# Column-tile streaming of the weights in the serial chain of a two-layer decode kernel

## The chip, the cores and the metric

The kernel runs on one core of one Trainium2 chip. The metric is device time of one execution in microseconds (us); three runs of the kernel before gave 1079.07, 1079.63 and 1081.63 us, a median of 1079.63 us. TensorE is called PE below, VectorE DVE, ScalarE ACT, GpSimd POOL, and SyncE, whose queue issues nearly all DMAs, SP. "PEld" is a weight load on PE: the stationary operand is loaded, then the moving operand is streamed past it.

## The reference

Two layers, each an attention block A over a cached K and V and a block B of small products, run one after the other on a single position of 8 batch rows. Both layers use the same cache and the same weights.

```python
B, Sq, D = 8, 1, 448;  Hq, Hkv, Sk, Dh = 16, 8, 4096, 256;  F = 1792
def _A_ref(x, k_cache, v_cache, wq, wo):
    q = (x @ wq) split into Hq heads of Dh
    scores = einsum("bhqd,bhkd->bhqk", q, k) * Dh ** -0.5   # k, v repeated to Hq heads
    o = einsum("bhqk,bhkd->bhqd", softmax(scores), v)
    return o.reshape(B, Sq, Hq * Dh) @ wo
def _B_ref(x, w1, w2, w3, w4):
    ...
    return x1 + _gelu(_layernorm(x1) @ w3) @ w4
x = A_x
x = x + _A_ref(_layernorm(x), A_k_cache, A_v_cache, A_wq, A_wo)
x = x + _B_ref(_layernorm(x), B_w1, B_w2, B_w3, B_w4)
x = x + _A_ref(_layernorm(x), A_k_cache, A_v_cache, A_wq, A_wo)
x = x + _B_ref(_layernorm(x), B_w1, B_w2, B_w3, B_w4)
```

With one position the shifts in block B move every column out of the row, so `hs` is zero, w1 and w2 drop out, and x1 is the block's own input, `_layernorm(x)`.

## The kernel before

**Work units.** A unit is a pass (0 for the first layer, 1 for the second), a batch row b and a pair of KV heads gp (0 to 3). Each unit has four K blocks and four V blocks of 1 MB; SBUF has 15 places of 1 MB for them (`NC = 15`). The second pass of a row reads the same cache as the first, so 12 of a row's 32 blocks stay in their places from pass 0 to pass 1 (`kept`: all K of gp 2 and 3, four V blocks), one more V block is parked in PSUM (`inner`) and a quarter of another (`part`). While a row's kept blocks wait for its second pass, three places are left through which other blocks stream.

**Order.** `block` and `first_kept` write out the order of all blocks (`items`). For a row, the two kept units of pass 0 come last before the turn to pass 1. Right after them come V blocks of other units that were saved up for this point: `items.extend(due[:n])`, with `AFTER = 11`. These are the `narrow` items; their loads are cut into two halves of 512 KB (`halved`). Rows 0 to 3 have 11 narrow V blocks here (they are also in `loose`), rows 4 to 7 have 10. Then come the scores of the same row's pass 1 with the kept K.

**The chain.** Between pass 0 and pass 1 of a row lies a serial chain for that row (`chain`, L499): `half` turns the attention output of the last two units into columns (o_sb copy L471, products L477, copy L481); `add_cols` multiplies by the second half of wo (L365, 64 products of a 128x128 weight block with a one-column vector); `norm` (DVE operations L227 to L302, a product with ones L235, a power on POOL L254); `mlp_hidden` with w3 (L383, 56 products) and gelu (L401 to L406); w4 (L365 again, 56); `norm` once more; `project_q` with wq (L316, 128) and the copy of q (L325); then `give_q` spreads q (L335, L339). In all these products the 128x128 block of the weights is the stationary operand and the vector is the moving one, so each output is a column with one number a partition, as the next step needs it.

**Interleaving.** The chain is a Python generator. `step` runs it to the next `yield` and so sets how its instructions stand between others in each engine's queue. In narrow items a step is taken after each half of a V block: `pv` (L847) issues 8 products of 128x8 weights with 256 moving columns, then comes a piece of chain, then the next 8. The four outputs of L847 stand on PSUM partitions 0, 32, 64 and 96, so four of them run in four column tiles of the array.

```python
            e["skip"] = got == 2 or (got == 3 and items[now[0]] in loose)
```

In narrow items `yield 0` goes straight on to the next piece, `yield 2` skips the next turn, and `yield 3` does so in loose items.

**Loads.** `emit_loads` issues a block's DMA (K L741 and L766, V L766, halves L769) when a place comes free; SP is one queue in order, and a half's DMA waits until PE has read what the place held.

**PSUM.** `sc` is the bank of the scores (L794, read by the exponentials L803 on ACT), `misc` holds the small results, `o` two accumulators of the attention output.

Of the kernel before, what the change touches and what calls it, by code (L numbers as in the profile page):

```python
# [17 lines left out]
def kernel(  # L18
# [72 lines left out]
    identb = consts.tile([128, 128], BF16, name="identb")  # L91
    nc.vector.tensor_copy(identb[:], ident)

    usel = consts.tile([128, 4], FP32, name="usel")
    for u in range(2):
        nc.vector.tensor_reduce(
            usel[:, 2 * u : 2 * u + 2],
# [10 lines left out]
        ALU.add,  # L108
    )

    ptz = consts.tile([128, 264], BF16, name="ptw")
    nc.vector.memset(ptz[:], 0.0)
    ptw = ptz[:, 0:256].rearrange("p (r n w) -> p r n w", r=2, w=8)
    psv_t = consts.tile([128, NP * 128], BF16, name="psv")
    psv = [
# [1 line left out]
        for k in range(NP)  # L117
    ]

    misc = psum.tile([128, 512], FP32, name="misc")  # L120
    ot_bank = misc[:, 256:288]
    sc = psum.tile([128, 512], FP32, name="sc")
# [15 lines left out]
        at, n = {"y": (0, 8), "st": (64, 2), "h": (80, HC), "q": (256, NB2)}[what]  # L138
        return store[0][:, at : at + n * nb]

    wv = consts.tile([128, 4], FP32, name="wv")
    nc.vector.memset(wv[:, 0:3], 1.0 / D)
    nc.vector.memset(wv[0:64, 3:4], 0.0)
    nc.vector.memset(wv[64:128, 3:4], 1.0 / D)
# [65 lines left out]
    def norm(x, nb, twice):  # L210

        def room(name, shape, at):
            n = shape[0] * shape[1]
            if nb < Bn:
                t = chn.tile([128, n * MID], FP32, tag=name)
                ap = t[:, 0 : n * nb]
            else:
                ap = scratch(at, n * nb)  # L220
            return ap.rearrange("p (s f b) -> p s f b", s=shape[0], f=shape[1])

        def bc(ap):
            return ap.unsqueeze(1).to_broadcast([128, 4, nb])

        xx = room("xx", (2, 4), 0)
        nc.vector.tensor_mul(xx[:, 0], x, wv[:].unsqueeze(2).to_broadcast([128, 4, nb]))  # L227
        nc.vector.tensor_mul(xx[:, 1], xx[:, 0], x)
        xs = room("xs", (1, 2), 512)[:, 0]
        nc.vector.tensor_reduce(  # L230
            xs, xx.rearrange("p s f b -> p s b f"), mybir.AxisListType.X, ALU.add
        )
        yield 3
        st = room_ps("st", nb).rearrange("p (s b) -> p s b", b=nb)
        nc.tensor.matmul(st, ones, xs, start=True, stop=True)  # L235
        yield 0
        mv = room("mv", (1, 2), 528)[:, 0]
        nc.vector.tensor_copy(mv, st)
        var = room("var", (1, 1), 608)[:, 0, 0]
        if nb == 1:  # L240
            nc.vector.scalar_tensor_tensor(
                var, mv[:, 0], mv[:, 0], mv[:, 1], ALU.mult, ALU.subtract, reverse1=True
            )
        else:
            nc.vector.tensor_mul(var, mv[:, 0], mv[:, 0])
            nc.vector.tensor_sub(var, mv[:, 1], var)

# [12 lines left out]

        if twice and nb == 1:
            nc.vector.scalar_tensor_tensor(
                ve[:, :, 0], var.to_broadcast([128, 2]), 0.0, eps2[:], ALU.max, ALU.add
            )
            power(0, 2)
        else:
            if twice:
                nc.vector.tensor_scalar(
                    ve[:, 1], var, 0.0, EPS * EPS / (1 + EPS), ALU.max, ALU.add
                )  # L270
                power(1, 2)
            nc.vector.tensor_scalar(ve[:, 0], var, 0.0, EPS, ALU.max, ALU.add)
            power(0, 1)
        xc = room("xc", (1, 4), 576)[:, 0]
        nc.vector.tensor_tensor(xc, x, bc(mv[:, 0]), ALU.subtract)  # L275
        yield 0
        if nb > 1:
            yield
        c = (1 + EPS) ** -0.5 if twice else 1.0
        rl = rs[:, n - 1]  # L280
        parts = ((0, 128, 0, 0, 3, 0), (0, 64, 64, 3, 4, 4), (64, 128, 64, 3, 4, 3))
        if nb == 1:
            nc.vector.scalar_tensor_tensor(
                xbs(1)[:, 0:4, 0], xc[:, :, 0], rl, low[:, int(twice)], ALU.mult, ALU.mult
            )
            parts = parts[1:2]
        for p0, p1, x0, f0, f1, to in parts:
            pp = slice(x0, x0 + p1 - p0)
            dst = xbs(nb)[p0:p1, to : to + f1 - f0, :]
            if nb == 1:  # L290
                nc.vector.tensor_scalar(dst, xc[pp, f0:f1], rl[pp], c, ALU.mult, ALU.mult)
            else:
                nc.vector.scalar_tensor_tensor(
                    dst,
                    xc[pp, f0:f1],
                    c,
                    rl[pp].unsqueeze(1).to_broadcast([p1 - p0, f1 - f0, nb]),
                    ALU.mult,
                    ALU.mult,
                )  # L300
# [43 lines left out]
    def y_room(nb):  # L344

        return room_ps("y", nb).rearrange("p (u f b) -> p u f b", u=2, b=nb)
# [29 lines left out]
    def mlp_hidden(b0, nb):  # L376

        yield from norm(xT[:, :, b0 : b0 + nb], nb, True)
        h_ps = room_ps("h", nb)
        for c in range(HC):  # L380
            for fc in range(4):
                w, xi = wblk(w3_sb, F, c, fc)
                nc.tensor.matmul(  # L383
                    h_ps[:, c * nb : c * nb + nb],
                    w,
                    xbs(nb)[:, xi, :],
                    start=(fc == 0),
                    stop=(fc == 3),
                )
            if c % 7 == 6:  # L390
                yield 0 if c == HC - 1 else None
        g_t = chn.tile([128, HC * MID], FP32, tag="g")
        hh = g_t[:, 0 : HC * nb]
        g0 = g_t[:, HC : 2 * HC] if nb == 1 else misc[:, 448 : 448 + HC * nb]
        if nb == 1:
            HT_t = chn.tile([128, HC, 1], BF16, tag="HT")
            HT = HT_t[:]
        else:
            HT = HTw[:, :, b0 : b0 + nb]

        nc.vector.tensor_scalar_mul(hh, h_ps, 0.5)  # L401
        nc.vector.scalar_tensor_tensor(g0, hh, 4 * 0.044715, hh, ALU.mult, ALU.mult)
        nc.vector.scalar_tensor_tensor(g0, g0, 1.0, hh, ALU.add, ALU.mult)
        nc.scalar.activation(g0, g0, ACT.Tanh, scale=2 * 0.7978845608028654)
        yield 0
        nc.vector.scalar_tensor_tensor(  # L406
            HT,
            g0.rearrange("p (c b) -> p c b", b=nb),
            1.0,
            hh.rearrange("p (c b) -> p c b", b=nb),  # L410
            ALU.add,
            ALU.mult,
        )
        yield 2
        return HT

    def mlp(b0, nb):
        HT = yield from mlp_hidden(b0, nb)
# [2 lines left out]
    def z_cols(zall, gps):  # L421
# [8 lines left out]
        nc.vector.tensor_tensor(  # L430
            zm[:],
            zs.unsqueeze(1).to_broadcast([128, 4, np_]),
            usel[:].unsqueeze(2).to_broadcast([128, 4, np_]),
            ALU.mult,
        )
        yield
# [12 lines left out]
                OT[:, j, h0 : h0 + 2], o_ps[:, j, h0 : h0 + 2], rz[:, 2 * u : 2 * u + 2, 0]  # L449
            )  # L450

    def half(o_ps, zall, gps, OT, ready):

        while locked:
            yield
# [11 lines left out]
        )  # L467
        while not ready():
            yield
        o_sb = chn.tile([128, Dh], FP32, tag="o_sb")  # L470
        nc.scalar.copy(o_sb[:], o_ps)  # L471
        yield
        nc.vector.memset(o_ps, 0.0)  # L473
        free_o.append(o_ps)
        ot_ps = ot_bank[:, 16 * g8 : 16 * g8 + 2 * n8].rearrange("p (j h) -> p j h", j=2)
        for j in range(2):
            nc.tensor.matmul(  # L477
                ot_ps[:, j], o_sb[:].rearrange("p (i j) -> p j i", j=2)[:, j], R, start=True, stop=True
            )
        yield 0  # L480
        nc.vector.tensor_copy(OT, ot_ps)  # L481
        locked.pop()
        yield

    locked = []
# [2 lines left out]
    def first_half(b, st, ready):  # L488
# [6 lines left out]
        xs = xT[:, :, b : b + 1]  # L495
        nc.vector.tensor_add(xs, xs, y_room(1)[:, 0])

    def chain(b, st, ready):
        OT = work.tile([128, 2, Hq // 2, 1], BF16, tag="OTb", bufs=1)  # L499
        yield from half(st["o", 1], st["z"], [2, 3], OT[:, :, :, 0], ready)  # L500
        yield from add_cols(
            y_room(1)[:, 1],
            lambda i: OT[:, i % 2, i // 2 - Hq // 2],
            wo_sb,
            range(NB2 // 2, NB2),
            2,
        )
        xs = xT[:, :, b : b + 1]
        nc.vector.tensor_add(xs, xs, y_room(1)[:, 1])
        yield from mlp(b, 1)  # L510
        qT = chn.tile([128, NB2], BF16, tag="qT2", bufs=2)
        yield from project_q(b, 1, qT[:].unsqueeze(2))
        state[1, b] = {"qT": qT}
        give_q((1, b))

# [445 lines left out]
    for idx, it in enumerate(items):  # L961
# [17 lines left out]
        if kv == 0:  # L979
# [32 lines left out]
                    scores(two[0], x, qbd, gp, between=turn)  # L1012
                    scores(two[1], x + 1, qbd, gp)
            if c == 1:
                p_n = work.tile([128, 4, 32, 4], BF16, tag="p_sb", bufs=1)
                p_of[n] = p_n
            if c % 2 == 1:
                exps(p_of[n], st["z"], gp, c // 2)
                if kept_now and c == 3:
# [152 lines left out]
```

## Time and profile before

| what | value |
|---|---|
| median of 3 runs | 1079.63 us |
| the profiled execution's own time | 1081.69 us |
| its span, first to last instruction | 1079.8 us |
| HBM read | 436.28 MB, 404 GB/s over the span |
| busy, share of the span | PE 61%, PEld 38%, DVE 57%, ACT 15%, POOL 2% |
| mean granted TensorE clock | 0.63 |
| chain products: L316 / L383 / L365 | 1024 / 448 / 1024 + 448 matmuls of one column |
| L847 | 3968 matmuls, 252.1 us busy, idle before them 116.5 us |
| L794 | 4896 matmuls, 246.6 us busy |

How to read it: "busy" is the time in which an engine executes; a line such as L847 is the line of the kernel that issued the instruction. The views used later are the page (totals, and the span in 40 slices), the chain of waits that ended last, the groups of instructions by line and form (busy time, mean duration of one in ns, idle time before them and what ended it), the timeline (start, duration, engine, line, operation, how many merged), the waits, and windows (busy time by engine in a chosen stretch, with the granted clock, the DMA share and GB/s).

### The profile page before, as it was taken

What the parts mean: (1) busy time and instruction counts of PE and PEld (TensorE: products, weight loads), DVE (VectorE), ACT (ScalarE), POOL (GpSimd) and SP (SyncE); (2) the same over time, 40 slices, a digit from 0 to 9 for tenths busy, and PEclk for the clock granted to TensorE, in tenths of its full rate; (3) what the DMA queues carried; (4) which work ended last, traced back from release to release, by engine and by line L of the source; (5) the groups of instructions that cost most, each with busy time, mean ns of one, the idle gap of its engine ahead of it and who ended that gap; (6) DMA issues with size and microseconds to landing.
All of it is one profiled execution on the core that took longest, in us unless ns stands there. A gap on an engine that the chain in (4) does not pass through costs nothing.

```text
span 1079.8 us, 29813 instructions
## 1 busy us (share of the span) xinstructions
PE 654.5 (61%) x13292; PEld 407.1 (38%) x13292; DVE 610.2 (57%) x1266; ACT 162.2 (15%) x612; POOL 16.3 (2%) x27
## 2 busy tenths in 40 slices
PE   3244458644776437764487537854776467756875
PEld 2122235422443214432254324532453245433554
DVE  4357841677426872368714773297429743874371
ACT  0001111111111111111112111111111111111110
POOL 0000000000000000000000000000000000000000
PEclk9999855656565565655556655665565556655665
DMA  9999999999999999999999999999999999999994
GB/s 359 394 425 425 425 407 390 424 424 424 389 393 426 424 423 396 407 426 422 422 394 420 421 425 397 393 426 426 410 395 425 424 407 399 425 424 406 393 419 179
DMA packets 69200, 438.22 MB, mean 406 GB/s; under 512 B 7368, under 2 KB 11344, under 8 KB 38736
## 3 DMA queue, kind: packets, MB, share of 16 engines
q1 hardware_dynamic: 68880, 435.94, 98.6%
q8 instruction: 104, 1.70, 0.6%
q10 hardware_dynamic: 192, 0.38, 0.1%
q14 instruction: 24, 0.20, 0.0%
HBM read 436.28 MB, written 0.01 MB: 404 GB/s over the span
## 4 chain that ended last, share of the span: by engine, by line
DMA 62%; PE 20%; DVE 11%; SPq 2%; issue 2%; ACT 2%; POOL 0%; DVEq 0%; ACTq 0%
DMA places<-in_A_v_cache_dram 35%; DMA places<-in_A_k_cache_dram 24%; PE o L847 7%; DVE places L779 7%; PE sc L794 6%; PE misc L365 2%; SPq L174 2%; PE misc L316 1%; DMA w_sb<-in_B_w_dram 1%; DVE store L814 1%; ACT p_n L803 1%; PE misc L477 1%; PE misc L383 1%; DVE places L821 1%; DMA wq_sb<-in_A_wq_dram 1%
## 5 line engine op out<-in xcount | busy, mean ns | idle before, releaser
L779 DVE STREAM_TRANSPOSE places<-places 128x512 uint32<-128x512 uint32 (+1 forms) x576 | 457.9, 855 | 127.7 <-DMA places<-in_A_k_cache_dram 125.7
L794 PE MATMUL sc<-places,qbd 128*8 128x256 bf16 (+1 forms) x4896 | 246.6, 352 | 243.2 <-DVE places L779 236.1
L847 PE MATMUL o<-places,ptw 128*8 128x256 bf16 x3968 | 252.1, 386 | 116.5 <-DMA places<-in_A_v_cache_dram 92.1
L794 PEld LDWEIGHTS <-qbd 128*8 128x8 bf16 x4896 | 129.2, 104 | 325.6 <-DVE places L779 145.9
L847 PEld LDWEIGHTS <-ptw 128*8 128x8 bf16 x3968 | 100.3, 101 | 184.7 <-issue 112.2
L803 ACT ACTIVATE p_n<-sc 128x256 bf16<-128x256 f32 x128 | 95.0, 742 | 381.6 <-PE sc L794 381.6
L957 ACT COPY ptw<-psv 128x32 bf16<-128x32 bf16 x248 | 52.7, 225 | 201.2 <-PE o L847 185.9
L837 ACT CAST psv<-misc 128x128 bf16<-128x128 f32 x64 | 17.0, 266 | 234.2 <-PE misc L830 234.2
L441 DVE RECIPROCAL rz<-misc 128x8 f32<-128x8 f32 (+1 forms) x35 | 6.6, 188 | 69.8 <-PE misc L438 69.8
L316 PEld LDWEIGHTS <-wq_sb 128*128 128x128 bf16 x1152 | 34.1, 104 | 27.2 <-issue 16.6
L365 PEld LDWEIGHTS <-wo_sb 128*128 128x128 bf16 x1280 | 37.8, 102 | 15.6 <-issue 15.4
L339 DVE CAST qbd<-misc 32x64 bf16<-32x64 f32 x104 | 22.4, 216 | 30.4 <-PE misc L335 29.4
L316 PE MATMUL misc<-xb,wq_sb 128*128 128x1 bf16 x1024 | 33.2, 166 | 3.1 <-issue 2.3
L477 PE MATMUL misc<-R_t,o_sb 128*128 128x8 f32 (+1 forms) x132 | 25.9, 305 | 13.4 <-ACT o_sb L471 7.1
L803 ACT ACTIVATION_READ_ACCUMULATOR p_n<-sc 128x1 f32 x128 | 33.6, 262 | 0.0
L365 PE MATMUL misc<-OT,wo_sb 128*128 128x1 bf16 x1024 | 31.5, 165 | 1.9 <-DVE OT L481 1.7
L477 PEld LDWEIGHTS misc<-R_t,o_sb 128*128 128x128 f32 x132 | 23.0, 245 | 24.4 <-ACT o_sb L471 14.2
L325 DVE CAST qT<-misc 128x32 bf16<-128x32 f32 x8 | 1.5, 191 | 51.8 <-PE misc L316 51.8
L254 POOL TENSOR_TENSOR t<-t,nhalf 128x2 f32<-128x2 f32 (+2 forms) x20 | 14.0, 703 | 1051.1 <-DVE t L275 1051.1
L473 DVE MEMSET o<- 128x256 f32 x33 | 9.0, 272 | 32.9 <-PE o L847 29.9
L830 PEld LDWEIGHTS <-p_n 128*128 128x128 bf16 x256 | 11.8, 105 | 31.5 <-issue 20.4
L830 PE MATMUL misc<-identb,p_n 128*128 128x32 bf16 x256 | 18.1, 191 | 8.1 <-ACT p_n L803 6.8
(107 smaller groups left out, 313.5 us busy)
## 6 DMA issues: line engine op xcount, KB each, us to landing
places<-in_A_k_cache_dram SPq DMA_DIRECT2D x65, 2048.0 KB, 19.1
places<-in_A_v_cache_dram SPq DMA_DIRECT2D x107, 1024.0 KB, 20.6
places<-in_A_v_cache_dram SPq DMA_DIRECT2D x202, 512.0 KB, 7.1
places<-in_A_k_cache_dram SPq DMA_DIRECT2D x62, 1024.0 KB, 13.2
places<-in_A_v_cache_dram SPq DMA_DIRECT2D x8, 768.0 KB, 14.3
wo_sb<-in_A_wo_dram SPq DMA_DIRECT2D x1, 3584.0 KB, 27.1
wq_sb<-in_A_wq_dram SPq DMA_DIRECT2D x3, 1024.0 KB, 9.7
w_sb<-in_B_w_dram SPq DMA_DIRECT2D x1, 1568.0 KB
```

Source lines behind the costliest of these rows:

```text
L174: nc.sync.dma_start(t[:, fc * cols : (fc + 1) * cols], src[fc * 128 : fc * 128 + 128, :])
L316: nc.tensor.matmul(q_ps[:, j * Hq + h, :], w, xbs(nb)[:, xi, :], start=(fc == 0), stop=(fc == 3),)
L339: nc.vector.tensor_copy(qbd[32 * a : 32 * a + 32, :, :, a, :], qs.rearrange("p e (f g u h) -> p (e f) u g h", f=2, u=2, h=2)[:, :, u],)
L365: nc.tensor.matmul(y_ps[:, fc, :], w[:, i, at : at + 128], rhs(i), start=start, stop=stop, skip_group_check=open is not None,)
L477: nc.tensor.matmul(ot_ps[:, j], o_sb[:].rearrange("p (i j) -> p j i", j=2)[:, j], R, start=True, stop=True)
L779: nc.vector.transpose(w, w)
L794: nc.tensor.matmul(sc[32 * k : 32 * k + 8, 128 * x : 128 * (x + nx)], qbd[:, ep, gp].rearrange("p a h -> p (a h)"), v, start=(n == 0), sto ...
L803: nc.scalar.activation(p_sb[:, :, :, 2 * u : 2 * u + 2].rearrange("p t i x -> p x t i"), sc[:, 256 * u : 256 * u + 256].rearrange("p (x t ...
L830: nc.tensor.matmul(pt_ps[:, t], p_sb[:, t].rearrange("p i x -> p (i x)"), cols, start=True, stop=True,)
L837: nc.scalar.copy(p_to, pt_ps.rearrange("p t k (a h) -> p a (t k) h", a=4))
L847: nc.tensor.matmul(o_ps[32 * q : 32 * q + 8, :], ptz[:, at : at + 8], v[:, y * Dh : (y + 1) * Dh], start=False, stop=(y >= 12), skip_group ...
L957: nc.scalar.copy(ptw[:, ring_of[it], :, 6:8], psv[slot_of[it[0]]][:, it[2]])
```

## The change

All of it is in the chain (`chain`); `first_half`, `rest` and the tail keep their products. The weights become the moving operand and the vector the stationary one, one column wide: a product gives a row on one PSUM partition. Four of them, on partitions 0, 32, 64 and 96 of the bank `sc`, run in four column tiles. wo's second half takes 16 products of 448 columns, w3 16 of 512 or 384 columns, w4 14 of 448, wq twice 16 of 512. After each such group DVE copies the bank to SBUF (`rows_out`, 128 x 448 or 512; for wq to bf16), and products with the copied rows as the stationary operand and a selection matrix as the moving one turn the rows into columns: for wo and w4 four fp32 products with `pick_all` (128x1, which also sums the four partial rows), for w3 four fp32 products with `pick` (128x4), for wq eight bf16 products with `pickb`. gelu works on 16 columns in place of 14.

Around it: one SBUF tile `buf` serves `o_sb`, the copied rows and the exponentials `p_of` in turn, and the lock that `half` takes is kept until wq's rows are turned (`hold=True`). The positions of the chain's yields change with the groups. The number of narrow items (`AFTER = 11`) and all loads stay.

```diff
+    nc.vector.tensor_copy(pick, ident.rearrange("p (q r) -> p q r", q=4)[:, :, 0])
...
+    pickb = ptz[:, 264:268]
+    nc.vector.tensor_copy(pickb, pick)
...
+    buf = consts.tile([128, 2 * Dh], FP32, name="buf")
...
+    nc.vector.tensor_reduce(pick_all, pick, mybir.AxisListType.X, ALU.add)
...
-    def half(o_ps, zall, gps, OT, ready):
+    def half(o_ps, zall, gps, OT, ready, hold=False):
...
-        o_sb = chn.tile([128, Dh], FP32, tag="o_sb")
-        nc.scalar.copy(o_sb[:], o_ps)
+        o_sb = buf[:, 0:Dh]
+        nc.scalar.copy(o_sb, o_ps)
...
-        locked.pop()
+        if not hold:
+            locked.pop()
...
+    def row(q, n):
+
+        return sc[32 * q : 32 * q + 1, 0:n]
+
+    def rows_out(n):
+
+        nc.vector.tensor_copy(buf[:, 0:n], sc[:, 0:n])
+
+    def sums(x, w, n, y_ps):
+
+        for i in range(n):
+            nc.tensor.matmul(
+                row(i % 4, D), x(i), w(i), start=i < 4, stop=i >= n - 4, skip_group_check=True
+            )
+        yield 0
+        rows_out(D)
+        yield
+        for fc in range(4):
+            nc.tensor.matmul(
+                y_ps[:, fc, :],
+                buf[:, min(128 * fc, D - 128) :][:, 0:128],
+                pick_all,
+                start=True,
+                stop=True,
+            )
+        yield 0
+
     def chain(b, st, ready):
         OT = work.tile([128, 2, Hq // 2, 1], BF16, tag="OTb", bufs=1)
-        yield from half(st["o", 1], st["z"], [2, 3], OT[:, :, :, 0], ready)
-        yield from add_cols(
-            y_room(1)[:, 1],
-            lambda i: OT[:, i % 2, i // 2 - Hq // 2],
-            wo_sb,
-            range(NB2 // 2, NB2),
-            2,
+        yield from half(st["o", 1], st["z"], [2, 3], OT[:, :, :, 0], ready, hold=True)
+        xs = xT[:, :, b : b + 1]
+        y_ps = y_room(1)[:, 1]
+        yield from sums(
+            lambda i: OT[:, i % 2, i // 2], lambda i: wo_sb[:, NB2 // 2 + i], NB2 // 2, y_ps
         )
-        xs = xT[:, :, b : b + 1]
-        nc.vector.tensor_add(xs, xs, y_room(1)[:, 1])
-        yield from mlp(b, 1)
+        nc.vector.tensor_add(xs, xs, y_ps)
+
+        yield from norm(xs, 1, True)
+        first, many = (0, 4, 7, 11), (4, 3, 4, 3)
+        for fc in range(4):
+            for q in range(4):
+                c, n = first[q], 128 * many[q]
...
+                nc.tensor.matmul(
+                    row(q, n),
+                    xbs(1)[:, xi, :],
+                    w,
+                    start=fc == 0,
+                    stop=fc == 3,
+                    skip_group_check=True,
+                )
+        yield 0
+        rows_out(512)
+        yield
+        h_ps = misc[:, 298:314]
+        for k in range(4):
+            nc.tensor.matmul(
+                h_ps[:, 4 * k : 4 * k + 4], buf[:, 128 * k : 128 * k + 128], pick, start=True, stop=True
+            )
+        yield 0
+        HT_t = chn.tile([128, 16, 1], BF16, tag="HT")
+        yield from gelu(h_ps, 16, 1, HT_t[:])
+        of = [4 * k + q for q in range(4) for k in range(many[q])]
+        yield from sums(lambda i: HT_t[:, of[i]], lambda i: w4_sb[:, i], HC, y_room(1)[:, 0])
+        nc.vector.tensor_add(xs, xs, y_room(1)[:, 0])
+
+        yield from norm(xs, 1, False)
+        q_ps = room_ps("q", 1)
+        rows = buf[:].bitcast(BF16)
+        for ph in range(2):
+            for fc in range(4):
+                for q in range(4):
...
+                    nc.tensor.matmul(
+                        row(q, 512),
+                        xbs(1)[:, xi, :],
+                        w,
+                        start=fc == 0,
+                        stop=fc == 3,
+                        skip_group_check=True,
+                    )
+            yield 0
+            nc.vector.tensor_copy(rows[:, 512 * ph : 512 * ph + 512], sc[:])
+            yield
+        for ph in range(2):
+            for k in range(4):
+                c = (k % 2) * Hq + 8 * ph + k // 2
+                nc.tensor.matmul(
+                    q_ps[:, c : c + 7 : 2],
+                    rows[:, 512 * ph + 128 * k : 512 * ph + 128 * k + 128],
+                    pickb,
+                    start=True,
+                    stop=True,
+                )
+        yield 0
+        locked.pop()
         qT = chn.tile([128, NB2], BF16, tag="qT2", bufs=2)
-        yield from project_q(b, 1, qT[:].unsqueeze(2))
+        nc.vector.tensor_copy(qT[:], q_ps)
+        yield
         state[1, b] = {"qT": qT}
         give_q((1, b))
...
-                p_n = work.tile([128, 4, 32, 4], BF16, tag="p_sb", bufs=1)
-                p_of[n] = p_n
+                p_of[n] = buf[:, Dh:].bitcast(BF16).rearrange("p (t i x) -> p t i x", t=4, i=32)
```

More of the change, by code (lines that the diff above doesn't have):

```diff
@@ L92 @@
     nc.vector.tensor_copy(identb[:], ident)
-    usel = consts.tile([128, 4], FP32, name="usel")
+    usel_t = consts.tile([128, 8], FP32, name="usel")
+    usel, pick = usel_t[:, 0:4], usel_t[:, 4:8]
     for u in range(2):
@@ L109 @@
     )
-    ptz = consts.tile([128, 264], BF16, name="ptw")
-    nc.vector.memset(ptz[:], 0.0)
+    nc.vector.tensor_copy(pick, ident.rearrange("p (q r) -> p q r", q=4)[:, :, 0])
+    ptz = consts.tile([128, 268], BF16, name="ptw")
+    nc.vector.memset(ptz[:, 0:264], 0.0)
+    pickb = ptz[:, 264:268]
+    nc.vector.tensor_copy(pickb, pick)
     ptw = ptz[:, 0:256].rearrange("p (r n w) -> p r n w", r=2, w=8)
@@ L139, in room_ps @@
         return store[0][:, at : at + n * nb]
-    wv = consts.tile([128, 4], FP32, name="wv")
+    wv_t = consts.tile([128, 5], FP32, name="wv")
+    wv, pick_all = wv_t[:, 0:4], wv_t[:, 4:5]
+    nc.vector.tensor_reduce(pick_all, pick, mybir.AxisListType.X, ALU.add)
     nc.vector.memset(wv[:, 0:3], 1.0 / D)
@@ L226, in norm @@
         xx = room("xx", (2, 4), 0)
-        nc.vector.tensor_mul(xx[:, 0], x, wv[:].unsqueeze(2).to_broadcast([128, 4, nb]))
+        nc.vector.tensor_mul(xx[:, 0], x, wv.unsqueeze(2).to_broadcast([128, 4, nb]))
         nc.vector.tensor_mul(xx[:, 1], xx[:, 0], x)
@@ L391, in mlp_hidden, with gelu @@
                 yield 0 if c == HC - 1 else None
+        HT = HTw[:, :, b0 : b0 + nb]
+        yield from gelu(h_ps, HC, nb, HT)
+        return HT
+    def gelu(h_ps, n, nb, HT):
         g_t = chn.tile([128, HC * MID], FP32, tag="g")
[L393 to L399, printed above, removed]
+        hh = g_t[:, 0 : n * nb]
+        g0 = g_t[:, n : 2 * n] if nb == 1 else misc[:, 448 : 448 + n * nb]
         nc.vector.tensor_scalar_mul(hh, h_ps, 0.5)
@@ L414, in mlp_hidden @@
         yield 2
-        return HT
     def mlp(b0, nb):
@@ L432, in z_cols @@
             zs.unsqueeze(1).to_broadcast([128, 4, np_]),
-            usel[:].unsqueeze(2).to_broadcast([128, 4, np_]),
+            usel.unsqueeze(2).to_broadcast([128, 4, np_]),
             ALU.mult,
@@ L477, in half @@
             nc.tensor.matmul(
-                ot_ps[:, j], o_sb[:].rearrange("p (i j) -> p j i", j=2)[:, j], R, start=True, stop=True
+                ot_ps[:, j], o_sb.rearrange("p (i j) -> p j i", j=2)[:, j], R, start=True, stop=True
             )
@@ new lines, in chain @@
+        xs = xT[:, :, b : b + 1]
+        y_ps = y_room(1)[:, 1]
+        yield from sums(
+            lambda i: OT[:, i % 2, i // 2], lambda i: wo_sb[:, NB2 // 2 + i], NB2 // 2, y_ps
+        )
+        nc.vector.tensor_add(xs, xs, y_ps)
[4 more added lines that the diff above has]
+                c, n = first[q], 128 * many[q]
+                if fc < 3:
+                    w, xi = w3_sb[:, fc * F + 128 * c : fc * F + 128 * c + n], fc
+                else:
+                    at = 3 * F + 128 * (c % 7)
+                    w, xi = w3_sb[:, at : at + n], 4 if c < 7 else 3
+                nc.tensor.matmul(
[6 more added lines that the diff above has]
+                )
@@ new lines, in chain @@
+        nc.vector.tensor_add(xs, xs, y_room(1)[:, 0])
[5 more added lines that the diff above has]
+                for q in range(4):
+                    at = 512 * (4 * ph + q)
+                    if fc < 3:
+                        w, xi = wq_sb[:, fc * HD + at : fc * HD + at + 512], fc
+                    else:
+                        w, xi = wq_sb[:, 3 * HD + 512 * q : 3 * HD + 512 * q + 512], 4 - ph
+                    nc.tensor.matmul(
[9 more added lines that the diff above has]
+            yield
```

## The prediction

> **What bounds the kernel now.** First the page, its slices:
>
> ```profile
> PEclk9999855656565565655556655665565556655665
> DMA  9999999999999999999999999999999999999994
> GB/s 359 394 425 425 425 407 390 424 424 424 389 393 426 424 423 396 407 426 422 422 394 420 421 425 397 393 426 426 410 395 425 424 407 399 425 424 406 393 419 179
> ```
>
> The DMA engines are occupied throughout; the rate is 425 GB/s at best and falls to some 390 in one or two slices of each of eight periods. The granted clock is near half for most of the span. Windows from the first narrow V half of a row to the first score of its second pass, for rows 1 and 7, put the dips where the chain runs:
>
> ```profile
> 283.78:312.10 28.32, 22.34 (x492) 14.28 (x495) 6.14 (x34) 2.37 (x12) 1.25 (x2) 0.56 1.00 385
> ...
> 988.27:1013.35 25.08, 21.51 (x476) 13.94 (x479) 6.13 (x34) 2.15 (x11) 1.24 (x2) 0.55 1.01 391
> ```
>
> The columns are length, PE, PEld, DVE, ACT, POOL, clock, DMA share, GB/s. Over the eight rows the length is 25.1 to 28.3 us. A half of a V block is 512 KB, 1.23 us at 425 GB/s: 22 halves (rows 0 to 3) need 27.1 us, 20 halves (rows 4 to 7) 24.6. So the stage is at most 2 us above what its bytes need, PE is busy for 79 to 86% of it, and in row 7 PE waits for landed V only 1.9 us. Chain and DMA are nearly in balance.
>
> How does a late chain reach the DMA? Three places of 1 MB stream here, so six halves are under way. For the tile `places` from 283 to 300 us the trace gives:
>
> ```profile
> DMA to landing us min/median/max: 6.1/7.8/8.2
> ```
>
> Six halves take 7.4 us at full rate; the fastest landing takes 6.1. After issue and reading little slack is left: a half that PE reads late by more than about 1 us sends its successor late, and a stage that ends x later moves the same bytes in x more. I count lengthening of the stage one for one.
>
> The chain itself, from row 7's timeline:
>
> ```profile
> 989.53 0.95 PE L365 MATMUL misc<-OT,wo_sb 128*128 128x1 bf16 x32
> ...
> 992.56 0.60 PE L847 MATMUL o<-places,ptw 128*8 128x256 bf16 x8
> 992.67 0.16 DVE L509 TENSOR_TENSOR xT<-xT,misc 128x4 f32<-128x4 f32 x1 [3.22 <-PE misc L365]
> ...
> 993.48 0.58 PE L235 MATMUL misc<-t,one 128*128 128x2 f32 x2 [0.32 <-DVE t L230]
> 993.99 0.30 PEld L847 LDWEIGHTS <-ptw 128*8 128x8 bf16 x9
> ...
> 995.86 1.05 PE L383 MATMUL misc<-xb,w_sb 128*128 128x1 bf16 x28 [0.51 <-DVE xb L283]
> ...
> 1010.75 0.19 DVE L325 CAST qT<-misc 128x32 bf16<-128x32 f32 x1 [5.42 <-PE misc L316]
> ```
>
> From wo's first product to q: 21.4 us. DVE starts 0.11 us after PE has gone on to the next V half.
>
> **Removed.** Ten portions. The start of a portion and of the V half behind it differ by 0.94 us for 32 products (wo twice, wq four times) and 0.83 for 28 (w3 and w4, twice each): 6 x 0.94 + 4 x 0.83 = 9.0 us of PE a chain. Each portion but a group's last had a V half of 0.53 us behind it, which now stands elsewhere.
>
> **Added streams.** Nearest rows: L847, four column tiles too, and its 16 products of 256 columns at half clock in the chain of waits; then fp32 products:
>
> ```profile
> 184.38 0.85 PE o L847 x16
> ```
>
> ```profile
> 543.11 1.02 PE L477 MATMUL misc<-R_t,o_sb 128*128 128x8 f32 x4
> ```
>
> A round of four is 0.213 us, so 0.373 for 448 columns and 0.427 for 512. wo: 4 rounds, 1.49; w3: 4 rounds at the pace of the longest, 1.71; w4: 14 products, 4 rounds, 1.49; wq: 8 rounds, 3.41. Together 8.1 us, 0.9 less than what goes; at full clock 4.05. If they did not overlap at all, 32.4.
>
> **Added copies.** PSUM to SBUF on DVE, by columns:
>
> ```profile
> L325 DVE CAST qT<-store 128x256 bf16<-128x256 f32 x1 | 0.4, 425 | 10.7 <-PE store L316 10.7
> ...
> L1137 DVE CAST places<-store 128x112 bf16<-128x112 f32 x1 | 0.3, 273 | 1.6 <-PE store L1128 1.6
> ```
>
> With L325's 191 ns for 32 columns that is 1.04 ns a column: 0.63 us for 448, 0.69 for 512. With 0.11 us before it and 0.06 behind (993.42 to 993.48, reduce to product) 0.80 and 0.86, five times. One V half (0.43 to 0.53) stands beside each; without it the whole copy is stall.
>
> **Added selection products.** An fp32 product is two records; two cost 0.51 us up to the next weight load (L235, 993.48 to 993.99), four 0.95 (L477, 543.11 to 544.06), so 0.22 each: eight records 1.8 us at half clock; at full clock L477's four take 0.64, L438's two 0.39, so 1.14. Three such groups: 5.4 us. wq's eight bf16 products: 8 x 0.03 + 0.17, 0.4.
>
> **The path, row 7, half clock.** wo 1.49 + 0.80 + 1.8 = 4.1; add and norm as now, 992.56 to 995.86, 3.3; w3 1.71 + 0.86 + 1.8 = 4.4; gelu 1.2 (998.21 to 999.36, and 0.06); w4 4.1; norm 3.15 (1001.99 to 1005.13); wq 2 x (1.71 + 0.86) + 0.4 + 0.3 = 5.85. Sum 26.1 against 21.4: +4.7. V halves left after q are four instead of three; they have landed, but the last one's place was freed six halves before, between wq's groups, and lands 6.1 us later at best: +0.3. Where the clock is up (wo's start, perhaps w4's or wq's end): -0.5. **+4.5 for rows 4 to 7.** In rows 0 to 3 two turns more are skipped, at 0.2 us each: 26.5. Row 3, at half clock throughout, takes 22.7 now (+3.8), row 0 24.2 (+2.3); rows 1 and 2 start at full clock, which takes 1.4 us from wo's part: 25.1 against 24.7 and 23.7 (+0.4, +1.4). With 0.6 for the last landing **+2.6 on average**: here waits of 3.1 to 5.8 us for landed V absorb part.
>
> **What else moves.** wq's streams beside V should raise the clock for the first scores, whose 32 products took 1.92 us at half clock and 1.11 at full: -0.5 a row, -4. The lock held longer: other users are held back by `alone` anyway until the scores; 0, and some 1 us a row if not. `buf` shared: exponentials already follow the scores, and these the chain, on PE; 0. Four small DVE operations at the start, under wq's load: 0, else 0.8 us. Fewer instructions: q8 fetches 1.70 MB, 0.6% of DMA time; a tenth of it, under 1 us. The DMAs keep order and number; SP waits for PE on the same halves, and behind a late half's wait stand all later loads.
>
> **Sum.** 4 x 4.5 + 4 x 2.6 - 4 = +24.4 us. The profiled execution took 1081.69 us, 1.9 around its span, 2.06 above the median: 1106.1 on its scale, **1104 us** on the median's.
>
> A rule against the change: the Trainium skill, "TensorE: Matmul & The Clock Gate", Measured speedup vs the span model, has three column tiles at 2.38 times, not 3. By it the streams take a quarter longer, 2.1 us a chain, and the estimate would be 1121; L847's 0.85 us shows all four at once, and I keep that.
>
> A rule for it: the skill's "TensorEngine Tiling", Key Properties, says that a change of tiling mode drains the engine. V halves cost 0.53 us beside full-array products and 0.43 among themselves, which agrees; five streams beside V halves would save some 1 us a chain, and the estimate would be 1096.
>
> **Rivals.** *The clock opens: faster.* These windows are 3.41 us long:
>
> ```profile
> 304.85:308.27 3.42, 3.14 (x88) 2.29 (x88) 0.00 (x0) 0.44 (x2) 0.00 (x0) 0.50 1.03 401
> ...
> 311.68:315.09 3.41, 2.98 (x56) 1.81 (x59) 0.00 (x0) 0.77 (x3) 0.00 (x0) 0.50 0.97 288
> 315.09:318.50 3.41, 2.33 (x59) 1.42 (x52) 0.37 (x2) 1.15 (x4) 0.00 (x0) 1.00 0.97 400
> ```
>
> PE was busier in the first, with 64 one-column products and 24 of V, and the clock stayed at half; the next-but-one streamed 56 x 256 = 14336 columns, and full clock followed. So columns streamed seem to decide. The new chain's best stretch outside wq (w4 with three V halves) has 12416, w3's and wo's less, and 1.8 us of selection follows each. If it suffices, the path is 2 x (0.75 + 0.80 + 1.14) + (0.86 + 0.86 + 1.14) + 4 x 0.86 + 0.6 + norms and gelu at 7.4 = 19.7 us, below today's 21.4: the V bytes bind, 0.5 us a row is won there, 0.8 at the scores, 8 x 1.3 = 10: 1069 us. It decides from about 12000 columns in each window on. The skill's page on the clock gate, Part 1, ties full clock to one sustained busy window; by it this is the case. The first window above speaks against a busy PE alone. Chance 0.10.
>
> *Hidden anyway.* The waits for landed V and the spare halves at the end absorb the longer path: 1080 us. Rows 0 to 3 speak for it, the 1.9 us in row 7 against. 0.11.
>
> *The columns do not overlap.* 24.3 us more a chain: about 1300. L847 speaks against. 0.01.
>
> *Worse than the sum.* Late halves starve the six in flight twice, in the chain and at the scores, 2 us a row more: 1120 to 1130. 0.08.
>
> **Numbers.** My forecast (0.70) covers 1086 to 1118. The range, 1080 to 1120, takes in the hidden case. 0.3% (3 us) is about what measurement tells from no change: faster 0.10, within 0.11, slower 0.79.
>
> **What would show it.** From o_sb to the first score 29 to 31 us in rows 4 to 7; groups of 16 wide products at 1.5 to 1.7 us; copies at 0.63 and 0.69; eight fp32 records at 1.8; PE's waits for landed V in the stage near zero, the dips deeper. I am wrong if the clock in the stage rises above 0.8 or the fp32 groups take under 1 us.

## The result and the profile after

The changed kernel takes 1119.38 us (median of 4 runs, 1115.02 to 1120.95) against 1079.35 for the kernel before in the same comparison: 1.0366 times as long, 95% interval 1.0345 to 1.0386. It is slower by 40 us, where +24.4 was forecast. The profiled execution took 1119.03 us with a span of 1117.2, 37.4 more than before.

The slices of the page, in the order in which those of before stand above:

```profile
PEclk9999867665565556865556556655566566656765
DMA  9999999999999999999999999999999999999994
GB/s 360 396 425 426 424 400 349 425 423 423 363 359 425 423 421 374 391 425 425 412 311 416 423 424 366 366 424 424 340 340 423 426 392 325 423 426 412 346 419 188
```

Between the dips the rate is 425 GB/s as before; the dips, 390 before, are now 311 to 374. So the time is lost where the chains run and just behind them. Against a steady 425 GB/s the eight stages (first narrow V half to first score) miss 48.6 us in place of 16.5, and the 20 us behind each stage 12.0 in place of 6.7, in all eight together. These two make 37.4 us, which is the whole difference of the spans. (A stretch misses its length times one minus its GB/s over 425: row 1's stage below 31.17 x (1 - 332 / 425) = 6.8 us.)

Windows of the stages of rows 1, 2, 5 and 7 (length, PE, PEld, DVE, ACT, POOL, clock, DMA share, GB/s):

```profile
286.86:318.03 31.17, 27.30 (x301) 15.13 (x304) 9.46 (x39) 2.37 (x12) 1.25 (x2) 0.50 0.93 332
420.90:448.70 27.80, 22.90 (x298) 12.89 (x301) 9.46 (x39) 2.37 (x12) 1.25 (x2) 0.69 0.98 366
...
791.86:822.00 30.14, 25.68 (x282) 14.13 (x285) 9.46 (x39) 2.15 (x11) 1.25 (x2) 0.53 0.84 297
1022.79:1049.14 26.35, 21.06 (x282) 11.13 (x285) 9.45 (x39) 2.14 (x11) 1.24 (x2) 0.74 0.97 363
```

Row 1 went from 28.3 to 31.2 us, row 5 from 25.4 to 30.1, row 7 from 25.1 to 26.4. The clock now differs from row to row: rows 1, 3 and 5 stay near half, the other five have 0.69 to 0.74. PE's timeline in row 5, with the clock at half, wo and w3 (lines of the changed kernel: L516 streams wo and w4, L552 w3; L511 copies; L523 and L565 are the fp32 selections; L946 is a V half, L868 its load):

```profile
793.73 1.70 PE L516 MATMUL sc<-wo_sb,OT 128*1 128x448 bf16 x16
795.23 0.64 PE L946 MATMUL o<-places,ptw 128*8 128x256 bf16 x8
796.17 1.87 PE L523 MATMUL misc<-wv,buf 128*128 128x1 f32 x8 [0.31 <-DVE buf L511]
797.97 0.60 PE L946 MATMUL o<-places,ptw 128*8 128x256 bf16 x8
...
801.28 1.87 PE L552 MATMUL sc<-w_sb,xb 128*1 128x512 bf16 x16 [0.85 <-DVE xb L290]
802.52 1.06 PE L946 MATMUL o<-places,ptw 128*8 128x256 bf16 x8
803.95 1.87 PE L565 MATMUL misc<-usel,buf 128*128 128x4 f32 x8 [0.38 <-DVE buf L511]
805.75 1.02 PE L946 MATMUL o<-places,ptw 128*8 128x256 bf16 x16
```

The streams of wo take 1.50 us up to the next V half (795.23 - 793.73); from there to the selection products are 0.94 us, of which the V half leaves 0.31 idle; the selections take 1.80. Behind w3's streams the V half begins after only 1.24 us (802.52 - 801.28), while the longer streams still run. In the 4.24 us from wo's streams to the V half behind the selections PE reads one V half; at 425 GB/s the DMA could have brought three.

What that does to the loads stands in the SP queue's waits, first before, then after, both for row 5's stage (us in total, times, longest):

```profile
SPq L769 <- PE o L847: 12.2, 15, 1.3
```

```profile
SPq L868 <- PE o L946: 22.8, 13, 2.7
```

For 22.8 of 30.1 us the queue of loads stood still because PE had not yet read a V half whose place the next load needs. The landing is not the cause: in this stage PE waited 0.6 us for landed V, and the loads landed sooner than before, which fits fewer of them under way. The tile `places` in row 5's stage, before and after:

```profile
DMA to landing us min/median/max: 6.6/7.0/7.8
```

```profile
DMA to landing us min/median/max: 4.1/5.6/7.0
```

### The profile page after: what moved, and what is told of

Same layout as the page of the kernel before. It is cut to its first block, busy times and chain, and to the rows that moved or that the text cites. A ratio compares the mean times of both kernels' runs of the same rounds, so it can differ in the third digit from the quotient of the medians.

```text
span 1117.2 us, 26759 instructions
## 1 busy us (share of the span) xinstructions
PE 667.6 (60%) x11740; PEld 399.6 (36%) x11740; DVE 636.4 (57%) x1309; ACT 161.8 (14%) x612; POOL 16.3 (1%) x27
## 4 chain that ended last, share of the span: by engine, by line
DMA 52%; PE 24%; DVE 16%; SPq 3%; issue 2%; ACT 2%; POOL 1%; DVEq 0%; ACTq 0%
DMA places<-in_A_v_cache_dram 28%; DMA places<-in_A_k_cache_dram 23%; DVE places L878 9%; PE o L946 6%; PE sc L893 5%; PE sc L586 2%; PE misc L523 2%; PE sc L516 2%; SPq L181 2%; DVE store L913 1%; DVE buf L511 1%; PE misc L565 1%; PE sc L552 1%; PE misc L483 1%; SPq L865 1%
## 5 line engine op out<-in xcount | busy, mean ns | idle before, releaser
L946 PE MATMUL o<-places,ptw 128*8 128x256 bf16 x3968 | 241.5, 372 | 118.6 <-DMA places<-in_A_v_cache_dram 94.8
L946 PEld LDWEIGHTS <-ptw 128*8 128x8 bf16 x3968 | 107.4, 105 | 196.6 <-issue 125.5
L902 ACT ACTIVATE buf<-sc 128x256 bf16<-128x256 f32 x128 | 94.9, 741 | 396.4 <-PE sc L893 396.4
L511 DVE COPY buf<-sc 128x448 f32<-128x448 f32 (+1 forms) x24 | 15.5, 646 | 36.2 <-PE sc L516 22.3
L483 PE MATMUL misc<-R_t,buf 128*128 128x8 f32 (+1 forms) x132 | 28.2, 323 | 12.8 <-ACT buf L477 7.1
L483 PEld LDWEIGHTS misc<-R_t,buf 128*128 128x128 f32 x132 | 25.3, 268 | 24.1 <-ACT buf L477 15.6
L586 PE MATMUL sc<-wq_sb,xb 128*1 128x512 bf16 x256 | 28.7, 597 | 8.5 <-DVE xb L290 5.5
L902 ACT ACTIVATION_READ_ACCUMULATOR buf<-sc 128x1 f32 x128 | 33.6, 263 | 0.0
L523 PE MATMUL misc<-wv,buf 128*128 128x1 f32 x128 | 25.8, 323 | 5.7 <-DVE buf L511 5.7
L523 PEld LDWEIGHTS misc<-wv,buf 128*128 128x128 f32 x128 | 24.4, 285 | 12.6 <-DVE buf L511 12.6
L372 PEld LDWEIGHTS <-wo_sb 128*128 128x128 bf16 x768 | 23.5, 104 | 12.8 <-issue 12.6
L929 PE MATMUL misc<-identb,buf 128*128 128x32 bf16 x256 | 18.2, 191 | 8.9 <-ACT buf L902 7.3
```

Of the source, the lines that this page charges most:

```text
L372: nc.tensor.matmul(y_ps[:, fc, :], w[:, i, at : at + 128], rhs(i), start=start, stop=stop, skip_group_check=open is not None,)
L483: nc.tensor.matmul(ot_ps[:, j], o_sb.rearrange("p (i j) -> p j i", j=2)[:, j], R, start=True, stop=True)
L511: nc.vector.tensor_copy(buf[:, 0:n], sc[:, 0:n])
L523: nc.tensor.matmul(y_ps[:, fc, :], buf[:, min(128 * fc, D - 128) :][:, 0:128], pick_all, start=True, stop=True,)
L586: nc.tensor.matmul(row(q, 512), xbs(1)[:, xi, :], w, start=fc == 0, stop=fc == 3, skip_group_check=True,)
L902: nc.scalar.activation(p_sb[:, :, :, 2 * u : 2 * u + 2].rearrange("p t i x -> p x t i"), sc[:, 256 * u : 256 * u + 256].rearrange("p (x t ...
```

## The experiments

Two theories were set against each other. **Halves**: with three places, a V half that is not read is a load that is not issued; a row loses the added length of its chain and, on top, 1.23 us for each V half that no longer stands inside the chain but behind it. wq's turns fell from four or five to three, so 12 V halves moved behind (148 to 136 in the eight chains). **Length**: only the length of the chain counts, and each us of it costs about 1.8 us, since 37.4 us of span stand against 21.2 us by which the stages got longer.

**Same work, V halves moved.** First the changed kernel with a turn more in each wq group:

```diff
                    nc.tensor.matmul(
                        row(q, 512),
...
                    )
+                if fc == 1:
+                    yield
```

> The changed kernel with one more turn in the middle of each of wq's two groups of 16 streams: two more V halves are read inside the chain of each row and two fewer after it; no instruction is added or dropped. Theory 'halves' (the loss of a row is the lengthening of its stage plus 1.23 us for each V half that the chain no longer reads, since with three places an unread half is an unissued load): up to 2 x 8 x 1.23 = 20 us come back, 1100 to 1110 us. Rival 'length' (only the length of the chain counts, and each us of it costs 1.8 us because late loads come due again at the scores): the work is the same, so 1116 to 1122 us.

Measured: 1108.57 us (1102.84 to 1113.71), 1.0245 (1.0201 to 1.0288) of before: 10.8 us less than the change, without an instruction added or dropped. By its profiled execution (1113.71 us) the stages miss 49.0 us, as many as in the change, and the 20 us behind each 6.9 in place of 12.0: what is won is won behind the stages. Then the reverse, in the kernel before:

```diff
-                if h % 8 == 7:
+                if h == Hq - 1 or (nb > 1 and h % 8 == 7):
                     yield (3, 0)[j] if h == Hq - 1 else None
```

> The kernel before, with wq's four portions of 32 products issued as two of 64: two fewer V halves stand in the chain of each row, which itself gets shorter by two halves of 0.53 us; nothing else changes. 'Halves': up to 20 us are lost, 1085 to 1099 us. 'Length': the chain is shorter by 1 us a row, so 1072 to 1081 us.

Measured: 1086.97 us, 1.0066 (1.0045 to 1.0088). The chain from wo's first product to q got shorter, 165.7 against 181.3 us over eight rows, and the kernel slower. "Length" falls with these two.

**The fp32 selections.** Rows copied as bf16, so that they are rounded, and turned by bf16 matrices:

```diff
-        nc.vector.tensor_copy(buf[:, 0:n], sc[:, 0:n])
+        nc.vector.tensor_copy(buf[:].bitcast(BF16)[:, 0:n], sc[:, 0:n])
...
-                buf[:, min(128 * fc, D - 128) :][:, 0:128],
-                pick_all,
+                buf[:].bitcast(BF16)[:, min(128 * fc, D - 128) :][:, 0:128],
+                pick_allb,
...
-                h_ps[:, 4 * k : 4 * k + 4], buf[:, 128 * k : 128 * k + 128], pick, start=True, stop=True
+                h_ps[:, 4 * k : 4 * k + 4], buf[:].bitcast(BF16)[:, 128 * k : 128 * k + 128], pickb, start=True, stop=True
```

> The changed kernel with the copied rows of wo, w3 and w4 rounded to bf16 and turned by bf16 selections, as wq's are. A group of four selections goes from 1.8 us (1.0 at full clock) to about 0.3: three groups a row, some 3.3 us a row in the mixture of clocks. 'Halves' (one for one): -26 us, about 1093 us. 'Length' (1.8 for one): -47 us, about 1072 us. If the fp32 selections are hidden by the wait for landed V: above 1110 us.

Measured: 1085.65 us (1081.36 to 1089.87), 1.0053 (1.0034 to 1.0071): 34 us less than the change, between the two expectations. Its windows for rows 1, 3, 4 and 6:

```profile
283.70:311.40 27.70, 20.19 (x286) 9.43 (x290) 9.45 (x39) 2.30 (x11) 1.25 (x2) 0.66 1.01 383
542.30:569.50 27.20, 16.93 (x288) 8.61 (x291) 9.46 (x39) 2.34 (x12) 1.25 (x2) 0.87 1.01 396
660.60:685.20 24.60, 16.09 (x270) 8.07 (x273) 9.46 (x39) 2.19 (x11) 1.25 (x2) 0.85 1.01 397
879.40:903.70 24.30, 16.44 (x271) 8.11 (x273) 9.45 (x39) 2.20 (x11) 1.25 (x2) 0.85 1.02 398
```

The path over eight rows falls by 34.5 us, to 165.3. From the start of a selection group to the next V half, the 24 groups take 38.2 us in the change (18 at 1.80, 6 at 0.98) and 8.8 here; so 29.4 of the 34.5 are the selections' own, which I had put at 26. The clock rises to 0.66 to 0.87 with them gone; it can account for the remaining 5 us, which is not shown apart. The opposite, each selection issued twice into the same place:

```diff
-        for fc in range(4):
+        for fc in (0, 1, 2, 3) * 2:
...
-        for k in range(4):
+        for k in (0, 1, 2, 3) * 2:
```

> The changed kernel with each of the twelve fp32 selection products of a row's chain issued twice into the same place. Each group gets 1.8 us longer at half clock, 0.9 at full: about 4.3 us a row. 'Halves': +34 us, about 1153 us. 'Length': +60 us, about 1180 us. If the stage has cover left: below 1135 us.

Measured: 1154.57 us, 1.0684 (1.0645 to 1.0724): +35.2 for 37.5 us of longer path, one for one.

**The change in two parts.** wo, w3 and w4 as before, wq alone as rows:

```diff
-        yield from sums(
-            lambda i: OT[:, i % 2, i // 2], lambda i: wo_sb[:, NB2 // 2 + i], NB2 // 2, y_ps
-        )
+        yield from add_cols(
+            y_room(1)[:, 1],
+            lambda i: OT[:, i % 2, i // 2 - Hq // 2],
+            wo_sb,
+            range(NB2 // 2, NB2),
+            2,
+        )
...
```

> The changed kernel with wo, w3 and w4 as they were before the change; only wq streams rows (with the shared buffer and the longer lock). wq's path is as long as before (some +0.2 us a row), but 12 V halves fewer are read in the eight chains. 'Halves': 12 x 1.23 + 2 = +16 us, about 1096 us. 'Length': 1.8 x 2 = +3, about 1083 us.

Measured: 1087.58 us, 1.0079 (1.0054 to 1.0104), between the two. The other part, with wq as before:

```diff
+        locked.pop()
         qT = chn.tile([128, NB2], BF16, tag="qT2", bufs=2)
+        yield from project_q(b, 1, qT[:].unsqueeze(2))
```

> The other part alone: wo, w3 and w4 stream rows, wq as before the change (and the lock given back before it). The number of V halves in the chains is that of before; the path is longer by what the whole change added to it less wq's share, some 16 us over eight rows. 'Halves': +16 to +20, 1095 to 1099 us, and with the wq part alone the sum makes up the whole change. 'Length': 1.8 x 16.5 = +30, about 1110 us.

Measured: 1117.87 us, 1.0346 (1.0313 to 1.0379). Both expectations were off, mostly for one reason: I had taken wq's path as unchanged. It is shorter. With wq alone the path over eight rows is 169.8 us, 11.5 below the 181.3 of before, and 8.5 of these in rows 0 to 3, where two V halves a row less stand in it; the other part alone has 211.0, 29.7 more. The two add up to +18.2, and the change has +18.5 (199.8). So wo, w3 and w4 cost nearly all of it: streams, copy and fp32 selection in each. With its path known, "halves" puts the other part at 1110 us; the 8 us on top go with the step in the table below.

**The buffer and the lock.** All products as before, with the shared `buf`, and the lock kept until q:

```diff
-        o_sb = chn.tile([128, Dh], FP32, tag="o_sb")
+        o_sb = buf[:, 0:Dh]
...
         yield from project_q(b, 1, qT[:].unsqueeze(2))
+        locked.pop()
```

> Only what stands around the streams: the shared buffer, the lock kept until q, the selection matrices; all products of the chain as before the change. Both theories: 1079 to 1082 us. If the lock or the shared buffer holds up other work: up to 1090 us.

Measured: 1079.67 us, 1.0006 (0.9990 to 1.0021). They cost nothing.

**The copies.** The changed kernel, each copy made by DVE and ACT together:

```diff
-        nc.vector.tensor_copy(buf[:, 0:n], sc[:, 0:n])
+        m = n // 2
+        nc.vector.tensor_copy(buf[:, 0:m], sc[:, 0:m])
+        nc.scalar.copy(buf[:, m:n], sc[:, m:n])
```

> The changed kernel with each of the five copies of a row's chain split in two halves that DVE and ACT make at once: about 0.3 us less each. If what a V half leaves uncovered of a copy lies on the chain: 8 to 12 us less than the changed kernel, 1107 to 1111 us. If the V half beside it covers it: 1117 to 1121 us.

Measured: 1113.58 us (1108.71 to 1124.38), 1.0336 (1.0274 to 1.0398): between the two expectations, and its four runs scatter around those of the change, so that no gain in time is shown. The path of its profiled execution, the fastest of the four, is 5.8 us shorter (194.0). How much of a copy the V half beside it covers stays open.

**Is there a version that gains?** Three tries with a short path and many V halves inside it. bf16 selections with the extra wq turns:

```diff
+                if fc == 1:
+                    yield
...
-        nc.vector.tensor_copy(buf[:, 0:n], sc[:, 0:n])
+        nc.vector.tensor_copy(buf[:].bitcast(BF16)[:, 0:n], sc[:, 0:n])
```

> Changed kernel with bf16 selections (the copied rows rounded to bf16) and one more turn in the middle of each wq group. The path is that of the run with bf16 selections and 16 V halves of 0.43 us more, 172 us in all, with 152 halves read in the chains. 'Halves': 172 - 152 x 1.23 = -15 against -1 of the kernel before, so up to 14 us below it if the DMA could follow; since it is then bound by its own rate and by the 6 us to land, 1070 to 1080 us. 'Length': the path is 9 us shorter than before, x 1.8: about 1063 us.

Measured: 1081.59 us, 1.0014 (0.9999 to 1.0029). With the copies split too:

```diff
-            nc.vector.tensor_copy(rows[:, 512 * ph : 512 * ph + 512], sc[:])
+            nc.vector.tensor_copy(rows[:, 512 * ph : 512 * ph + 256], sc[:, 0:256])
+            nc.scalar.copy(rows[:, 512 * ph + 256 : 512 * ph + 512], sc[:, 256:512])
```

> As the run before in this call, and each copy of the rows split between DVE and ACT: 0.80 and 0.86 us become about 0.5, five times a row, 13 us over eight rows where no V half covered it (some 5 to 8 are left). 'Halves': the DMA is the bound already, so within 4 us of the run before. 'Length': 8 x 1.8, 14 us less than it.

Measured: 1080.28 us, 1.0013 (0.9996 to 1.0030). wq alone with the extra turns, the diffs of both as above:

> wq alone streams rows, with a turn more in the middle of each of its groups: no fp32 selection is left, and the V halves read in the chains are 16 more than with wq alone. 'Halves': path about 177 us, 152 halves, 177 - 187 = -10; below about zero the loss stays at the 21 to 24 us that kernels with -1 to -7 have, so 1076 to 1081 us. 'Length': the path is 7 us longer than with wq alone, so 1087 us or more.

Measured: 1079.65 us, 1.0003 (0.9985 to 1.0020). And the kernel before with more turns:

```diff
             range(NB2 // 2, NB2),
-            2,
+            1,
         )
```

> The kernel before with wo's two portions of 32 products issued as four of 16: 16 V halves more in the chains, no other change. 'Halves' with a floor: the stage is bound by its loads already, 1077 to 1081 us. Without a floor: 12 us less, about 1067 us. 'Length': 7 us more path, 1086 us or more.

Measured: 1079.54 us, 1.0005 (0.9991 to 1.0019). None of these can be told from the kernel before. There is a floor: in the stages of the kernel before the DMA engines are occupied (share 1.00 to 1.02) at 385 to 403 GB/s, in those of the change they are not (0.84 to 0.98). No run changed the number of places or the size of the loads, so what sets the floor's height is not tested.

**All kernels in one table.** Path: wo's first product to the end of q's copy, summed over eight rows of the profiled execution; halves: V halves that PE read from the stage's start to there; x = path - 1.23 x halves. The last column is the profiled execution's own time, from which path and halves come; the median is over all runs.

| kernel | path | halves | x | median us | profiled us |
|---|---|---|---|---|---|
| selections twice | 237.3 | 136 | 70 | 1154.57 | 1154.85 |
| the change | 199.8 | 136 | 32.5 | 1119.38 | 1119.03 |
| without wq | 211.0 | 147.5 | 29.6 | 1117.87 | 1119.39 |
| split copies | 194.0 | 136 | 26.7 | 1113.58 | 1108.71 |
| more wq turns | 205.7 | 149.5 | 21.8 | 1108.57 | 1113.71 |
| before, fewer wq turns | 165.7 | 131.5 | 4.0 | 1086.97 | 1086.97 |
| wq only | 169.8 | 136 | 2.5 | 1087.58 | 1088.41 |
| before | 181.3 | 148 | -0.7 | 1079.35 | 1081.69 |
| bf16 selections | 165.3 | 136 | -2.0 | 1085.65 | 1081.36 |
| buffer and lock | 178.6 | 148 | -3.4 | 1079.67 | 1079.68 |
| bf16, more wq turns | 176.6 | 148 | -5.4 | 1081.59 | 1080.79 |
| the same, split copies | 176.8 | 149 | -6.6 | 1080.28 | 1078.72 |
| before, finer wo | 193.4 | 163 | -7.1 | 1079.54 | 1077.08 |
| wq only, more turns | 173.6 | 147 | -7.2 | 1079.65 | 1081.90 |

From x = 2.5 to 70 the median is 1085 to 1088 us plus x for every kernel but one, which is 1083 plus x; the profiled executions' own times lie at 1082 to 1092 plus x, so the line holds to about 5 us. Below about -3 the median stays at 1080 to 1082, whatever the path. Between the two is a soft corner, where the kernel before stands. The median of bf16 selections lies 5 us above its neighbours there, but the x of -2.0 is that of its profiled execution, the fastest of ten, which took 1081.36 us and lies with them; what the paths of the slower ones were is not on record. By path alone the table has no order: 205.7 is faster than 199.8, and 165.7 slower than 193.4.

## Why the prediction was right, and where it was off

*Way and place: right; size: at the edge.* The kernel is slower, and 32.1 of the 37.4 us between the two profiled executions are lost in the eight stages, by chain length against 512 KB halves, as forecast. But 1119.38 us lies above the 1086 to 1118 of my forecast and 0.6 us inside the end of the range, and that it is no further off is partly luck: terms that were too high (the path) and too low (V halves, first scores) offset each other.

*Durations at half clock: right.* Row 5's path is 26.4 us, against 26.1 in the sum for rows 4 to 7; rows 1 and 3 have 26.5, the 26.5 forecast for the half-clock rows of 0 to 3. Streams of wo 1.49 forecast and 1.50 measured, selections 1.8 and 1.80, copies 0.63 and 0.69 against these groups:

```profile
L511 DVE COPY buf<-sc 128x448 f32<-128x448 f32 x16 | 10.0, 624 | 24.1 <-PE sc L516 22.3 <-PE o L946 1.8
...
L511 DVE COPY buf<-sc 128x512 f32<-128x512 f32 x8 | 5.5, 691 | 12.2 <-PE o L946 10.7 <-PE sc L552 1.5
```

The step from stream to selection is 0.94 and not 0.80, because the copy starts 0.26 us after the V half has begun (795.49 on DVE), not 0.11.

*The clock: too low.* I took 0.5 us a row for it; five rows ran at 0.69 to 0.74, and their paths are 23.0 to 24.6 us; six of the 24 selection groups took 0.98 us in place of 1.80. The path grew by 18.5 us, not by the 24.7 of my terms (4 x 4.7 - 4 x 0.5 for rows 4 to 7, and 2.3 + 0.4 + 1.4 + 3.8).

*The V halves behind the chain: mis-sized, and this is the step that made the forecast low.* "They have landed", I wrote, and took 0.3 us a row, 0.6 in rows 0 to 3, for the last landing, 3.6 in all. But a half that lies landed and unread holds one of three places. Twelve halves left the chains, and 12 x 1.23 = 14.8 us is what their loads take. With the path, 18.5 + 14.8 = 33.3, of the 37.4 us between the two profiled executions, whose paths these are. The sentence that "a stage that ends x later moves the same bytes in x more" missed it too: the stages grew by 21.2 us, but miss 32.1 us more at 425 GB/s, so loads worth 10.9 us fall behind them. The four halves at their end are read in one burst, and their successors' loads come after it.

*The first scores: wrong.* -4 us was taken for the higher clock. The 20 us behind the stages lose 5.3 us more instead, which is part of the 37.4 above and not on top of it. In row 7 PE waits 1.22 us for V behind the first scores. By the order of the loads this is the half issued at 1046.06, and the last two issues up to it came 3.0 and 2.5 us after the one before; the corresponding two of the kernel before came 2.1 and 1.5 us after theirs.

The remaining 4 us (6 or 7 by the medians) are the corner of the table: the kernel before sits just where path and loads balance, and the kernels with x above 2 lie 3 to 8 us over 1080 plus x, at 2.5 as at 70. Why this step comes at once is open.

*The rivals.* "Hidden anyway" is refuted by the two runs with selections taken away and doubled. "The clock opens" came about in part, and in the run with bf16 selections nearly fully; there the path fell to 165.3 us and the profiled execution's time only to 1081.36: the 10 us that this rival promised below today's time aren't there, because the DMA engines are occupied in these stages (share 1.01 or 1.02 in the four shown). "Worse than the sum", at 1120 to 1130, came nearest: late halves do cost a second time, but by the loads they hold back.

*The two rules.* Four column tiles ran at once, each at its own pace: in row 5's wo the products start in fours, 0.373 us apart, and in w3 the tiles with 384 columns go on every 0.32 us beside those with 512 every 0.427. The Trainium skill gives 2.38 times for three column tiles ("TensorE: Matmul & The Clock Gate", Measured speedup vs the span model). No run here has three tiles, or one at a time, so that figure is not tested; the streams were not a quarter longer than forecast, 1.50 us against 1.49. A V half before a stream takes 0.38 us (793.35 to 793.73 in row 5), one before full-array products took 0.53; that agrees with the Trainium skill's "TensorEngine Tiling", Key Properties, on draining, and is small beside the rest.

## What to carry to other kernels

Where a serial chain is woven into a stream of loads through few places, count two things: its length, and how many loads' worth of reading stands inside it. In these runs their difference against the load rate was lost, above a floor. Fewer, longer pieces can lose by the second even where they win by the first. Turning a row into columns costs a copy and a product each time; with fp32 operands that is more here (0.94 + 1.80 us at half clock) than a 64-block matrix-vector product that needs no turning (2 x 0.94).

## What the runs showed of the hardware

An fp32 selection with one or four moving columns costs the same, 1.80 us for four at half clock, a bf16 one a fraction (four in 0.27 us, row 5). While PE was busy for 85% of row 5's stage, its clock stayed at half; with the fp32 pauses removed PE was busy for 65% of row 4's stage and had 0.85. So the clock did not go with occupation. It went with the columns streamed: the traces give the clock in steps of 3.41 us, and in those of the kernel before and of the change no step with fewer than 2592 columns (products in four column tiles counted at a quarter) was followed by full clock, and none with more than 3104 by half (in all fourteen traces 10 of some 4000 steps lie outside these bounds). PE's busy share was as low as 0.48 before a step of full clock, and up to 1.00 before one of half. And a half of 512 KB landed 4.1 us after its issue at best, not 6.1: so what I had read as the landing's own time was in part, as it seems, the queue of the other halves.
